# Computing a Q piece of a segment as one 16-head matmul group, so that only the last K is cut in two

## The chip, the cores and the metric

The kernel runs on one core of one Trainium2 chip. The metric is device time in microseconds (us). A "pair" below is one TensorE weight load with its matmul. Every single time here is of a run in the fast state (granted TensorE clock 0.989 to 0.999). Ratios are the mean time of a kernel's fast runs over that of the kernel before's fast runs on the same chip, so they are not quite the ratios of the medians that stand beside them. "The first chip" below is that of the first call, the one of before and after; its number is not on record, and three of before's four times and its trace existed before the changed kernel was shown, so that all of them ran on one chip is assumed. The kernel before itself took 922 to 925 us on the numbered chips and 933 us on the first; so kernels are compared through their ratio, and with kernels of the same call where possible.

## The reference, cut to what matters

An attention layer that runs over 64 segments one after the other, because the first 8 rows of a segment's input (the memory) are the output of the segment before; then a gated MLP over all rows, which the change does not touch.

```python
for s in range(n_seg):                               # 64 segments of 32 rows, D = 512
    h = jnp.concatenate([mem, xs], axis=1)           # 8 memory rows + 32 rows
    q = jnp.einsum('btd,dhe->bhte', h, Wq)           # 32 heads of 128
    k = jnp.einsum('btd,dhe->bhte', h, Wk)
    v = jnp.einsum('btd,dhe->bhte', h, Wv)
    scores = jnp.where(mask, jnp.einsum('bhqe,bhke->bhqk', q, k) * scale, -1e9)
    o = jnp.einsum('bhqk,bhke->bhqe', _softmax(scores), v)
    o = jnp.einsum('bhte,hed->btd', o, Wo)
    mem = o[:, :M, :].copy()                         # feeds the next segment
```

## The kernel before

A segment goes through these stages on TensorE: Q and K of all heads; scores of the heads 0 to 15 (half 0); V; scores of half 1; the sums of the softmax; PV of both halves; the output product; the memory rows, which are copied into the next segment's input `hT`. PV is the product of the softmax's weights with V. "Filler" below is Q, K and V work for rows of later segments that don't depend on the memory (lines 404 and 423); it is put where TensorE would otherwise wait. Q and K come in pieces. A piece is a run of matmuls into one PSUM bank (4 parts of the contraction times 4 column groups of the array), an eviction by ScalarE into `Tst`, and a transpose by VectorE into `QT` or `KT`:

```python
    QKP = ((0, 0, 8, (0, 1)), (1, 0, 4, (6, 7)), (1, 4, 4, (3, 2)))    # half, first pair of heads, pairs of heads, banks of Q and K

    def QK(s, piece, mi):                    # mi 0: Q, 1: K
        b, p0, np_, banks = piece
        ...
        h0, nh = 16 * b + 2 * p0, 2 * np_
        for dc in range(DC):                 # 4 parts of the contraction
            for c in range(4):               # 4 column groups of the array, side by side
                rhs = ws[:, dc, :].rearrange("p (h c i) -> p c h i", c=4, i=32)[:, c, h0:h0 + nh, :]
                pe(lambda e, ...: e.matmul(ps[32 * c:32 * c + 32, bank, 0:32 * nh], lhsT=hT[:, sl, dc, :], rhs=rhs,
                                           start=(dc == 0), stop=(dc == DC - 1), tile_position=(0, 32 * c)), ...)

    def QK_evac(piece, mi):
        ...
        act(lambda e: e.activation(out=st_..., in_=ps[:, bank, 0:64 * np_]..., func=ACT.Copy), ...)    # ScalarE: bank -> Tst
        ...
        dve(lambda e: e.transpose(out=dst, in_=src), ...)                                               # VectorE: Tst -> QT or KT

    for s in range(NSEG):
        ...
        for piece in QKP:
            for mi in range(2):
                QK(s, piece, mi)
                QK_evac(piece, mi)
        S_half(s, 0); sm_exp(0)
        V_half(s, 0, (0, 1, 2))
        S_half(s, 1)                         # needs the last K transpose
        sm_sums(0); sm_exp(1); sm_ln(0)
        V_half(s, 0, (3,)); V_evac(0, "dve")
        V_half(s, 1, gs=(0, 2)); V_evac(1, "dve", (0, 2))
        sm_sums(1); sm_rcp(0); sm_ln(1); sm_rcp(1)
        V_half(s, 1, gs=(2, 4)); V_evac(1, "act", (2, 4))
        sm_norm(0); sm_norm(1)
        ...                                  # PV, output product, memory rows (work of segment 0 alone is left out above)
```

A 16-head piece has 16 pairs of 512 columns; an 8-head piece 16 pairs of 256. The stage has 32 pairs of 512 and 64 of 256.

## Time and profile before

| | before |
|---|---|
| time, median (4 runs) | 933.11 us (930.78 to 934.89) |
| profiled execution | 925.72 us, core span 923.8 us |
| segment (first Q/K matmul to the next one's), median | 10.75 us |
| Q/K stage, first to last matmul start, median | 3.384 us |

Three places of the page: the busy time, the queue that brings the program, and the chain that ended last. In the queue's line stand the transfers, the MB and their share of 16 engines' span. "issue" in the chain is time in which the engine waited for nothing that the profile shows.

```profile
PE 875.5 (95%) x24038; PEld 572.1 (62%) x24045; DVE 458.0 (50%) x1098; ACT 461.4 (50%) x1281; POOL 155.3 (17%) x408
...
q8 instruction: 190, 3.11, 1.5%
...
PE 89%; DVE 3%; ACT 2%; DMA 2%; issue 2%; SPq 1%; POOL 0%; ACTq 0%
...
L477 PE MATMUL f_ps<-f_arena,f_hT 128*32 128x512 bf16 (+1 forms) x6144 | 233.9, 308 | 0.7 <-ACT f_hT L649 0.6
L489 ACT ACTIVATE f_Tst<-f_ps 128x256 bf16<-128x256 f32 (+1 forms) x384 | 155.7, 453 | 90.0 <-PE f_ps L477 70.9
```

TensorE bounds the kernel (busy for 95% of the span, 89% of the chain), and the Q/K matmuls (line 477) are its largest group (233.9 us).

### The profile page before, as it was taken

The page shows a single profiled execution, that of the slowest core. Times are in us where ns is not written, and L with a number is a line of the kernel's source. Part 1 is how long each engine was busy: PE and PEld are TensorE (multiplying, and loading weights), DVE is VectorE, ACT ScalarE, POOL GpSimd, SP SyncE. Part 2 cuts the span into 40 slices and gives each one's busy share as a digit, 9 for nine tenths or more (in the row PEclk, how much of TensorE's full clock was granted, in tenths as well). Part 3 has the DMA queues.
Part 4 walks back from the last instruction along what each step waited for, and adds up shares of the span by engine and source line. Part 5 has one row for each costly group of instructions (what it writes and reads, how often), then busy time and mean ns, then how long its engine had stood idle before and what let it go on. Part 6 is the DMA issues. An engine that isn't in the chain of part 4 may idle for free.

```text
span 923.8 us, 51830 instructions
## 1 busy us (share of the span) xinstructions
PE 875.5 (95%) x24038; PEld 572.1 (62%) x24045; DVE 458.0 (50%) x1098; ACT 461.4 (50%) x1281; POOL 155.3 (17%) x408
## 2 busy tenths in 40 slices
PE   6979999999999999999999999899989899999998
PEld 6756667776776777676676777566666544444443
DVE  3434555555554555455555555444445454453433
ACT  2436566666565665556565556555565655400000
POOL 1421111111111111111112111211111122200000
PEclk9999999999999999999999999999999999999999
DMA  9952322122303222222312020413132393021201
GB/s 321 376 154 59 66 52 62 42 50 64 73 19 75 44 56 44 50 61 38 50 44 68 26 78 22 118 27 84 39 55 51 68 269 120 1 98 49 84 12 36
DMA packets 103405, 71.69 MB, mean 78 GB/s; under 512 B 62120, under 2 KB 88688, under 8 KB 103184
## 3 DMA queue, kind: packets, MB, share of 16 engines
q1 hardware_dynamic: 102672, 68.06, 28.2%
q8 instruction: 190, 3.11, 1.5%
q14 instruction: 31, 0.25, 0.1%
q0 software_dynamic: 192, 0.20, 0.1%
q10 hardware_dynamic: 320, 0.07, 0.0%
HBM read 39.46 MB, written 18.61 MB: 63 GB/s over the span
## 4 chain that ended last, share of the span: by engine, by line
PE 89%; DVE 3%; ACT 2%; DMA 2%; issue 2%; SPq 1%; POOL 0%; ACTq 0%
PE f_ps L477 24%; PE f_ps L627 13%; PE f_ps L575 11%; PE f_ps L1025 10%; PE f_ps L404 6%; PE f_ps L594 3%; PE f_ps L671 3%; PE f_ps L423 3%; PE f_ps L987 3%; PE f_ps L1018 3%; PE f_ps L1095 2%; PE f_ps L646 2%; PE f_ps L520 2%; DVE f_V_sb L586 2%; PE f_ps L511 1%
## 5 line engine op out<-in xcount | busy, mean ns | idle before, releaser
L477 PE MATMUL f_ps<-f_arena,f_hT 128*32 128x512 bf16 (+1 forms) x6144 | 233.9, 308 | 0.7 <-ACT f_hT L649 0.6
L477 PEld LDWEIGHTS f_ps<-f_arena,f_hT 128*32 128x32 bf16 x6144 | 160.6, 97 | 77.1 <-ACT f_hT L649 16.6
L489 ACT ACTIVATE f_Tst<-f_ps 128x256 bf16<-128x256 f32 (+1 forms) x384 | 155.7, 453 | 90.0 <-PE f_ps L477 70.9
L575 PE MATMUL f_ps<-f_arena,f_hT 128*32 128x256 bf16 (+1 forms) x3072 | 142.2, 308 | 3.1 <-issue 3.0
L497 DVE STREAM_TRANSPOSE f_QT<-f_Tst 128x128 uint32<-128x128 uint32 (+1 forms) x192 | 65.8, 343 | 155.8 <-ACT f_Tst L489 155.8
L627 PE MATMUL f_ps<-f_arena,f_cT 128*32 128x384 bf16 (+1 forms) x4096 | 125.8, 274 | 9.3 <-ACT f_cT L613 8.7
L627 PEld LDWEIGHTS f_ps<-f_arena,f_cT 128*32 128x32 bf16 x4096 | 85.1, 97 | 52.0 <-ACT f_cT L613 20.9
L565 POOL TENSOR_TENSOR f_E_sb<-f_R_sb,f_E_sb 128x64 bf16<-128x64 f32 x128 | 43.8, 342 | 437.1 <-ACT f_R_sb L557 437.1
L1025 PE MATMUL f_ps<-f_arena 128*128 128x512 bf16 x448 | 101.3, 379 | 2.5 <-DVE f_arena L1031 1.6
L497 DVE STREAM_TRANSPOSE f_KT<-f_Tst 128x128 uint32<-128x128 uint32 (+1 forms) x192 | 68.4, 356 | 46.3 <-ACT f_Tst L489 46.3
L586 DVE TENSOR_SCALAR f_V_sb<-f_ps 128x512 bf16<-128x512 f32 (+1 forms) x128 | 65.9, 553 | 49.1 <-PE f_ps L575 49.0
L639 ACT ACTIVATE f_part<-f_ps 128x384 bf16<-128x384 f32 (+1 forms) x128 | 46.4, 384 | 83.9 <-PE f_ps L627 83.9
L575 PEld LDWEIGHTS f_ps<-f_arena,f_hT 128*32 128x32 bf16 x3072 | 68.7, 96 | 19.5 <-issue 5.1
L615 DVE TENSOR_SCALAR f_cT<-f_ps 128x320 bf16<-128x320 f32 x128 | 56.9, 486 | 47.1 <-PE f_ps L600 47.1
L1025 PEld LDWEIGHTS f_ps<-f_arena 128*128 128x128 bf16 x448 | 43.5, 98 | 56.0 <-DVE f_arena L1031 2.6
L404 PE MATMUL f_ps<-f_hTe,f_arena 128*128 128x128 bf16 x1024 | 72.6, 222 | 1.5 <-DMA f_arena<-in_A_Wk_dram 1.3
L613 ACT ACTIVATE f_cT<-f_ps 128x320 bf16<-128x320 f32 x128 | 49.0, 435 | 48.3 <-PE f_ps L600 48.3
L404 PEld LDWEIGHTS f_ps<-f_hTe,f_arena 128*128 128x128 bf16 x1024 | 58.5, 99 | 12.0 <-issue 10.1
L534 ACT ACTIVATE f_E_sb<-f_ps 128x224 bf16<-128x224 f32 x128 | 45.4, 355 | 35.8 <-PE f_ps L526 34.6
L594 PE MATMUL f_ps<-f_E_sb,f_V_sb 32*128 32x40 bf16 x2048 | 41.5, 178 | 8.9 <-DVE f_E_sb L561 5.7
L1031 DVE TENSOR_TENSOR f_arena<-f_ps,f_arena 128x512 f32<-128x512 f32 x28 | 19.3, 690 | 57.9 <-PE f_ps L1025 57.9
L557 ACT ACTIVATE f_R_sb<-f_R_sb 128x160 f32<-128x160 f32 x128 | 43.1, 337 | 4.4 <-ACT f_part L435 0.4
(103 smaller groups left out, 1052.6 us busy)
## 6 DMA issues: line engine op xcount, KB each, us to landing
wT_d<-f_wst SPq DMA_DIRECT2D x32, 256.0 KB, 3.4
f_arena<-wT_d SPq DMA_DIRECT2D x32, 256.0 KB, 4.6
f_arena<-in_A_Wq_dram SPq DMA_DIRECT2D x4, 1024.0 KB, 9.1
f_arena<-in_A_Wk_dram SPq DMA_DIRECT2D x4, 1024.0 KB, 14.3
f_arena<-in_A_Wv_dram SPq DMA_DIRECT2D x4, 1024.0 KB, 14.9
f_arena<-in_A_Wo_dram SPq DMA_DIRECT2D x4, 1024.0 KB, 13.7
f_Vx<-vext_d SPq DMA_DIRECT2D x62, 64.0 KB, 3.0
vext_d<-f_Vs SPq DMA_DIRECT2D x24, 128.0 KB, 2.2
```

What stands on the lines that cost most here:

```text
L404: pe(lambda e, h=h, dc=dc, hh=hh: e.matmul(ps[:, bank, hh * 128:(hh + 1) * 128], lhsT=ws[:, dc, h * DH:(h + 1) * DH], rhs=hTe[:, ck % 3, d ...
L477: pe(lambda e, dc=dc, c=c, rhs=rhs: e.matmul(ps[32 * c:32 * c + 32, bank, 0:32 * nh], lhsT=hT[:, sl, dc, :], rhs=rhs, start=(dc == 0), sto ...
L489: act(lambda e: e.activation(out=st_.rearrange("p (hp i r) -> p hp i r", i=32, r=2), in_=ps[:, bank, 0:64 * np_].rearrange("p (hp r i) -> ...
L497: dve(lambda e: e.transpose(out=dst, in_=src), reads=tok, writes=[(nm, b, k) for k in halves(b, p0, np_)])
L575: pe(lambda e, dc=dc, c=c, c0=c0: e.matmul(ps[32 * c:32 * c + 32, bank, 0:w], lhsT=hT[:, sl, dc, :], rhs=w_v[:, dc, c0:c0 + w], start=(dc ...
L586: dve(lambda e: e.tensor_scalar(out=dst, in0=src, scalar1=VSC, scalar2=None, op0=ALU.mult), reads=[PB(bank)], writes=tok)
L594: pe(lambda e, q=q, c=c, g=g, c0=c0: e.matmul(ps[:, PVB[c], c0:c0 + 40], lhsT=V_sb[q, b, g * 128:(g + 1) * 128], rhs=E_sb[q, b, g * 40:(g ...
L613: act(lambda e: e.activation(out=dst, in_=src, func=ACT.Copy, scale=UNSC), reads=[PB(PVB[c])], writes=[("cT", c)])
L615: dve(lambda e: e.tensor_scalar(out=dst, in0=src, scalar1=UNSC, scalar2=None, op0=ALU.mult), reads=[PB(PVB[c])], writes=[("cT", c)])
L627: pe(lambda e, h=h, g=g, i=i, b=b, c=c: e.matmul(ps[32 * g:32 * g + 32, bank, 0:d1 - d0], lhsT=cTh[:, i, 8:40], rhs=w_o[:, h, d0:d1], star ...
L639: act(lambda e: e.activation(out=part[:, s % 8, d0:d1], in_=ps[:, bank, 0:d1 - d0], func=ACT.Copy), reads=[PB(bank)], writes=[("part", s % ...
L1025: pe(lambda e: e.matmul(ps[:, bank, 0:TB], lhsT=z2[:, sc, fb * 128:(fb + 1) * 128], rhs=wTb[tb % 2][:, :, sc, :], start=(sc == 0), stop=(s ...
```

## The change

Its intent: the same columns in fewer instructions, none of the change in the stretch where the softmax's latency is exposed. The Q piece of half 1 becomes one 16-head piece; only the last K stays in two, so that the last eviction and transpose before the scores remain small (in before about 380 and 311 ns at 256 columns, 597 and 445 ns at 512). Per segment: 80 pairs in place of 96, 5 evictions and 5 transposes in place of 6, and no Q/K piece in bank 3.

```diff
-    QKP = ((0, 0, 8, (0, 1)), (1, 0, 4, (6, 7)), (1, 4, 4, (3, 2)))
+    QKP = ((0, 0, 8, 0, 0), (0, 0, 8, 1, 1), (1, 0, 8, 0, 6), (1, 0, 4, 1, 7), (1, 4, 4, 1, 2))
...
-    def QK(s, piece, mi):
-        b, p0, np_, banks = piece
+    def QK(s, piece):
+        b, p0, np_, mi, bank = piece
...
         for piece in QKP:
-            for mi in range(2):
-                QK(s, piece, mi)
-                lastop["qk"[mi]] = em.by_eng["pe"][-1]
-                QK_evac(piece, mi)
+            QK(s, piece)
+            lastop["qk"[piece[3]]] = em.by_eng["pe"][-1]
+            QK_evac(piece)
```

More of the change, by code (lines that the diff above doesn't have):

```diff
@@ L466, in fast_path @@
     VXB = 5
-    def QK(s, piece, mi):
-        b, p0, np_, banks = piece
+    def QK(s, piece):
+        b, p0, np_, mi, bank = piece
         ws = (w_q, w_k)[mi]
-        bank = banks[mi]
         sl = slot(s)
@@ L482, in halves, with QK_evac @@
         return range(p0 // 4, (p0 + np_) // 4)
-    def QK_evac(piece, mi):
-        b, p0, np_, banks = piece
-        bank = banks[mi]
+    def QK_evac(piece):
+        b, p0, np_, mi, bank = piece
         st_ = Tst[:, mi, 64 * p0:64 * (p0 + np_)]
```

## The prediction

> **What bounds the kernel.** The page's busy shares give PE 95% (875.5 of 923.8 us), ACT 50%, DVE 50%; the chain of waits that ended last is 89% PE. Most of the span is 64 serial segments (median 10.6 to 10.9 us from one segment's first Q/K matmul to the next one's). The granted clock is 0.998. PE's stream of columns, plus PE's waits inside a segment, set the time.
>
> **What the change does.** A segment's Q/K stage has 32 pairs of 512 columns and 64 of 256 before, 48 and 32 after. Columns are the same 32,768; 16 pairs go (1,024 of 24,038 matmuls), with one ScalarE eviction and one VectorE transpose a segment. The softmax, V, PV and output parts keep their order on every engine. The last piece (256-column K, eviction, transpose) keeps its size; only banks change, and those written next have been evicted long before.
>
> **Cost on PE, from the timeline's start times.** Four column groups run side by side: starts 3 to 4 ns apart inside a group of four, then one column sweep. A group of four takes about 217 ns at 512 columns and 109.2 ns at 256, so two 256 groups cost 218.4: the weight loads (about 97 ns each) are hidden. [...] Four 512 groups in place of eight 256 groups save 6 to 10 ns a segment. The "16 fewer pairs" are 17% of the stage's pairs but about 0.2% of its 3.38 us.
>
> **The eviction chain.** The second score half starts 55 ns after the last K transpose, about 40 ns after PE could have gone. In before, the last K eviction starts 51 ns after its last matmul ends: it waits only for PE, not for ScalarE's backlog. For after I estimate starts from the segment's first Q/K matmul with trace durations (eviction 512: 597 ns, 494 to the next; 256: about 380, 280 to the next; transpose 445 and 311[...]): Q eviction 2.83 us, first K half 3.32, last K 3.70 (before: 3.71); transposes 3.46, 3.83, 4.11 (before: last at 4.12). So the score half gains under 10 ns; the backlog that the change clears was hidden. ScalarE's and VectorE's saved work lies off the critical path. The later waits (PV on the normalised E, output product on the context eviction, memory rows on ScalarE) move along unchanged.
>
> **Sum.** 5 to 10 ns a segment x 64 = 0.3 to 0.6 us, below the 4 us spread of the three runs before.
>
> Predicted: 932.4 us, range 929.0 to 935.5. Faster by over 2%: 1%; within 2%: 98%; slower by over 2%: 1%.
>
> **What the profile would show.** Right: 23,014 matmuls; first to last Q/K matmul start falls by about 10 ns from 3.38 us; 320 Q/K evictions and transposes; ScalarE and VectorE each 4 to 10 us less busy with the span unchanged; last K eviction still about 50 ns after its matmuls; second score half at 4.48 us; median segment within 20 ns. Wrong: the Q/K stage shortens by over 50 ns (pairs had a price of their own), or the last transpose queues behind the larger Q transpose, which moves the second score half by up to 50 ns (+3 us, still within 2%).
>
> **What would make it wrong.** Instruction fetch on PE, if the scattered "issue" stalls (2% of the chain) scale with the number of instructions: about 1 us. The exposed transpose queue. [...]

The sum stands at 5 to 10 ns a segment, 0.3 to 0.6 us in all. Before's trace gives the steps from start to start: 216.7 ns for a group of four at 512 columns (mean; median 216), 109.2 ns at 256; for queued transposes 0.37 us after one of 128x256 uint32, 0.28 us after one of 128x128. The starts laid out above use only the first of these two.

## More of the kernel before

The experiments ran in calls of several kernels each, on different chips (named by number where known).

The program is fully unrolled: 24,038 matmuls stand one after the other in TensorE's instruction stream.

## The result, and the profile after

The changed kernel took 919.45 us (918.16 to 921.66, 4 runs) against 933.11 us: a ratio of 0.9858, 95% interval 0.9828 to 0.9887. That is within 2%, but 13 us below the predicted 932.4 and outside its range. The core spans of the profiled executions differ by less, 923.8 and 916.0 us.

The same lines of the page for the changed kernel:

```profile
PE 874.1 (95%) x23021; PEld 544.1 (59%) x23021; DVE 449.2 (49%) x1034; ACT 461.1 (50%) x1217; POOL 155.1 (17%) x408
...
q8 instruction: 182, 2.98, 1.4%
...
PE 92%; DVE 3%; ACT 2%; DMA 1%; issue 1%; SPq 0%; POOL 0%
...
L476 PE MATMUL f_ps<-f_arena,f_hT 128*32 128x512 bf16 (+1 forms) x5120 | 233.4, 337 | 0.7 <-ACT f_hT L647 0.7
L487 ACT ACTIVATE f_Tst<-f_ps 128x512 bf16<-128x512 f32 (+1 forms) x320 | 156.7, 510 | 88.5 <-PE f_ps L476 88.4
```

The Q/K matmuls take the same busy time (233.4 against 233.9 us), and so do the evictions. What has moved is "issue" in the chain, 2% to 1%, and the instruction transfers, 190 to 182: eight of 16,384 bytes less for the 1,024 pairs, 2,048 instructions, that were removed: 64 bytes an instruction.

I laid the two traces beside each other, with times from the first Q/K matmul of each segment (medians of the segments):

| | before | after | predicted for after |
|---|---|---|---|
| last Q/K matmul starts | 3.384 us | 3.374 us | about 10 ns earlier |
| eviction of the last K starts | 3.71 us | 3.70 us | 3.70 us |
| transpose of the last K starts | 4.12 us | 4.11 us | 4.11 us |
| second score half starts | 4.49 us | 4.48 us | 4.48 us |
| shortest segment | 10.556 us | 10.543 us | 5 to 10 ns less |
| median segment | 10.75 us | 10.58 us | within 20 ns |
| the 62 segments after the first, together | 671.5 us | 662.6 us | 0.3 to 0.6 us less |

Every step inside an undisturbed segment came out as laid out. But few segments of before were undisturbed. Sorted into kinds with the same side work, each segment's excess over the shortest of its kind adds up to 12.2 us before and 4.3 us after (other ways of sorting move this by some 0.3 us). So the gain is not in the segment's schedule; it lies in something that lengthens single segments at irregular places.

One such place in before, from the timeline. The columns are start, length, engine, line, operation, out and in with shapes, count, and in brackets how long the engine had been idle and what ended it:

```profile
369.62 0.11 PEld L575 LDWEIGHTS f_ps<-f_arena,f_hT 128*32 128x32 bf16 x4
...
369.65 0.28 PE L575 MATMUL f_ps<-f_arena,f_hT 128*32 128x256 bf16 x4
...
370.51 0.23 PEld L575 LDWEIGHTS f_ps<-f_arena,f_hT 128*32 128x32 bf16 x12 [0.79 <-issue]
370.51 0.51 PE L575 MATMUL f_ps<-f_arena,f_hT 128*32 128x256 bf16 x12 [0.58 <-issue]
```

This is a V quarter: 16 pairs of one kind, with no semaphore between them. Four go, then TensorE stands still for 0.8 us, then twelve go. No other engine holds it up.

Over the whole run such waits show in the list of waits of the weight loads. The columns are who waited, for what, us in total, times, and the longest. Before:

```profile
PEld f_ps L404 <- issue: 10.1, 41, 1.5
PEld f_ps L575 <- issue: 5.1, 8, 1.5
...
PEld f_ps L594 <- issue: 2.6, 6, 1.2
...
PEld f_ps L627 <- issue: 2.5, 10, 0.5
...
PEld f_ps L541 <- issue: 1.4, 3, 0.5
```

and after:

```profile
PEld f_ps L404 <- issue: 10.8, 43, 0.8
...
PEld f_ps L625 <- issue: 2.2, 10, 0.5
...
PEld f_ps L592 <- issue: 1.1, 2, 0.6
...
PEld f_ps L573 <- issue: 0.3, 1, 0.3
```

The first line of each (some 0.25 us a time, at filler matmuls that use the whole array after column tiles) is much the same in both, and so is that of line 627 (625 in the changed kernel); a wait that stays like this does not explain the gain. The other lines shown go from 9.1 to 1.4 us. All "issue" waits of the weight loads but the first line, those not shown included, go from 15.8 to 7.5 us.

I then numbered TensorE's trace records and looked where over 0.4 us pass from one record's start to the next one's, between 150 and 730 us, at an instruction that waits on no semaphore. These I call long stops; their lengths include the ordinary step from one record to the next. For before:

```
record number    16833 17345 19649 22465 22721 23489 25281 26049 26305 28353 36801 42177
modulo 256         193   193   193   193   193   193   193   193   193   193   193   193
```

All twelve stand a multiple of 256 instructions apart, and 256 instructions of 64 bytes are 16,384 bytes, the size of every one of the 190 transfers of the instruction queue (before has 48,223 TensorE records, 254 a transfer). The changed kernel has four such stops, all at 193 modulo 256 too. At the twelve stops of before, the block's transfer had landed 1.26 to 1.59 us before its first instruction ran, and 3.5 to 4.5 us (median 3.9) lay between the first instruction of the block before and that of the late one.

That gives theory A. TensorE's program is brought in blocks of 256 instructions, and where blocks are used up faster than the next ones come, TensorE stops. In the middle of the loop (with filler work) a segment of before has 722 TensorE records in about 10.7 us, so a block lasts 10.7 x 256/722 = 3.8 us on average: inside the range of 3.5 to 4.5 us that passed at the stops. After the change it is 690, 4.0 us a block. And some stretches are denser than the average. The range is not a limit for a single block: 36 of before's 149 blocks between 150 and 730 us took less than 3.5 us from start to start (the shortest 2.87), so blocks can also follow each other faster. What tells a late block is its landing. In the traces of before, the changed kernel, e1, e3 and e9 no block's first instruction started, in that stretch, less than 1.1 us after the last transfer had landed. All twelve stops of before stand at blocks whose transfer had landed less than 1.6 us before, and so do the long stops at block starts of all other traces but one (in e1, 2.1 us). Of all blocks, 64 of 149 had landed so late in before, and 24 of 144 in the changed kernel.

Most block starts made no long stop: 137 of the 149 between 150 and 730 us in before, and 140 of 144 in the changed kernel.

The rivals. Theory B: the sixth eviction and transpose cost the time. Theory C: the banks did, since a Q piece of before shared bank 3 with filler work. Theory D, which the prediction named: a pair has a price of its own on the array.

### The profile page after: what moved, and what is told of

Its sections match the earlier page's. It is cut to its first block, busy times and chain, and to the rows that moved or that the text cites. A ratio compares the mean times of both kernels' runs of the same rounds, so it can differ in the third digit from the quotient of the medians.

```text
span 916.0 us, 49661 instructions
## 1 busy us (share of the span) xinstructions
PE 874.1 (95%) x23021; PEld 544.1 (59%) x23021; DVE 449.2 (49%) x1034; ACT 461.1 (50%) x1217; POOL 155.1 (17%) x408
## 4 chain that ended last, share of the span: by engine, by line
PE 92%; DVE 3%; ACT 2%; DMA 1%; issue 1%; SPq 0%; POOL 0%
PE f_ps L476 24%; PE f_ps L625 13%; PE f_ps L573 11%; PE f_ps L1022 10%; PE f_ps L404 7%; PE f_ps L592 3%; PE f_ps L669 3%; PE f_ps L423 3%; PE f_ps L984 3%; PE f_ps L1015 3%; PE f_ps L1092 3%; PE f_ps L518 2%; DVE f_V_sb L584 2%; PE f_ps L644 2%; PE f_ps L509 1%; PE f_ps L598 1%
## 5 line engine op out<-in xcount | busy, mean ns | idle before, releaser
L476 PE MATMUL f_ps<-f_arena,f_hT 128*32 128x512 bf16 (+1 forms) x5120 | 233.4, 337 | 0.7 <-ACT f_hT L647 0.7
L487 ACT ACTIVATE f_Tst<-f_ps 128x512 bf16<-128x512 f32 (+1 forms) x320 | 156.7, 510 | 88.5 <-PE f_ps L476 88.4
L476 PEld LDWEIGHTS f_ps<-f_arena,f_hT 128*32 128x32 bf16 x5120 | 132.8, 97 | 104.1 <-ACT f_hT L647 16.2
L495 DVE STREAM_TRANSPOSE f_QT<-f_Tst 128x256 uint32<-128x256 uint32 x128 | 57.0, 445 | 181.7 <-ACT f_Tst L487 181.7
L573 PE MATMUL f_ps<-f_arena,f_hT 128*32 128x256 bf16 (+1 forms) x3072 | 140.1, 308 | 0.0
L495 DVE STREAM_TRANSPOSE f_KT<-f_Tst 128x128 uint32<-128x128 uint32 (+1 forms) x192 | 65.8, 343 | 27.7 <-ACT f_Tst L487 26.3
L573 PEld LDWEIGHTS f_ps<-f_arena,f_hT 128*32 128x32 bf16 x3072 | 67.2, 96 | 15.3 <-issue 0.3
L532 ACT ACTIVATE f_E_sb<-f_ps 128x224 bf16<-128x224 f32 x128 | 45.4, 355 | 35.8 <-PE f_ps L524 34.6
## 6 DMA issues: line engine op xcount, KB each, us to landing
f_arena<-in_A_Wo_dram SPq DMA_DIRECT2D x4, 1024.0 KB, 13.6
```

Of the source, the lines that this page charges most:

```text
L476: pe(lambda e, dc=dc, c=c, rhs=rhs: e.matmul(ps[32 * c:32 * c + 32, bank, 0:32 * nh], lhsT=hT[:, sl, dc, :], rhs=rhs, start=(dc == 0), sto ...
L487: act(lambda e: e.activation(out=st_.rearrange("p (hp i r) -> p hp i r", i=32, r=2), in_=ps[:, bank, 0:64 * np_].rearrange("p (hp r i) -> ...
L495: dve(lambda e: e.transpose(out=dst, in_=src), reads=tok, writes=[(nm, b, k) for k in halves(b, p0, np_)])
L573: pe(lambda e, dc=dc, c=c, c0=c0: e.matmul(ps[32 * c:32 * c + 32, bank, 0:w], lhsT=hT[:, sl, dc, :], rhs=w_v[:, dc, c0:c0 + w], start=(dc ...
```

## The experiments

Thirteen runs were made (e5 and e13 are the changed kernel itself). Stops are counted as above (over 0.4 us, no semaphore, 150 to 730 us, in the profiled execution). "wT" is the spatial weight of the MLP, which the kernel transposes by transfers in the background of the segment loop.

| run | chip | pairs in Q/K, evictions | instruction transfers | stops, us | us | ratio to before |
|---|---|---|---|---|---|---|
| before | | 96, 6 | 190 | 12, 7.5 | 933.11 | 1 |
| after | | 80, 5 | 182 | 4, 2.7 | 919.45 | 0.9858 |
| e1 pairs back | 12 | 96, 5 | 190 | 8, 5.1 | 924.39 | 1.0019 |
| e2 six evictions | 12 | 80, 6 | 182 | 3, 2.3 | 916.64 | 0.9944 |
| e3 128 pairs | 12 | 128, 5 | 206 | 45, 35.8 | 966.49 | 1.0494 |
| e4 before, no wT | 12 | 96, 6 | 190 | 0 | 919.32 | 0.9966 |
| e5 after again | 7 | 80, 5 | 182 | 4, 2.9 | 917.16 | 0.9917 |
| e6 no-operations | 7 | 80, 5 | 182 | 5, 3.1 | 918.73 | 0.9933 |
| e7 V whole | 7 | 80, 5 | 174 | 1, 1.0 | 918.70 | 0.9942 |
| e8 K whole | 7 | 64, 4 | 174 | 2, 1.1 | 936.01 | 1.0128 |
| e9 96 more loads | 12 | 80, 5 | 206 | 45, 37.3 | 967.76 | 1.0483 |
| e10 after, no wT | 12 | 80, 5 | 182 | 0 | 916.07 | 0.9937 |
| e11 memory rows in 4 | 12 | 80, 5 | 176 | 5, 3.9 | 924.59 | 1.0029 |
| e12 V split one to three | 11 | 80, 5 | 174 | 2, 1.5 | 920.69 | 0.9968 |
| e13 after again | 11 | 80, 5 | 182 | 5, 3.0 | 917.96 | 0.9933 |

Before took 922.2 to 922.4 us on chip 12, 924.6 on chip 7 and 922.7 on chip 11. Every stop in the table but one of e11's five stands at the first instruction of a block of 256.

### e1: the pairs back, everything else of the change kept

```diff
-        for dc in range(DC):
-            for c in range(4):
+        cuts = ((0, 8), (8, 16)) if (b, mi) == (1, 0) else ((0, nh),)
+        for u0, u1 in cuts:                  # two column halves of the same bank
+            for dc in range(DC):
+                for c in range(4):
```

> The changed kernel, but its second Q piece is computed as two 256-column halves into its one bank: 96 pairs a segment as before, with the 5 evictions, 5 transposes and the banks of the changed kernel. Theory A (TensorE is short of instructions: its program is brought in 16 KB blocks of 256 instructions, and a block that is used up faster than the next one arrives stops it): back to the time of before, 928 to 935 us. Theory B (fewer evictions and transposes gave the time): stays at 918 to 921. Theory C (the banks gave it, as no Q piece shares bank 3 with the filler any more): stays at 918 to 921.

Measured: 924.39 us against 922.22 us for before on this chip, ratio 1.0019 (0.9992 to 1.0046). The absolute numbers were expected for a chip on which before takes 933; in the ratio, with the 16 pairs back, the whole gain is gone, although evictions, transposes and banks are those of the changed kernel. Theories B and C each expected the gain to stay.

### e2: six evictions and transposes, 80 pairs

```diff
+        if (b, mi) == (1, 0):                # the Q piece of half 1: evict and transpose 256 columns at a time
+            for k in range(2):
+                QK_evac1((b, 4 * k, 4, mi, bank), 256 * k)
+        else:
+            QK_evac1(piece, 0)
```

> The changed kernel with its 80 pairs and banks, but the second Q piece is evicted and transposed in two halves, so 6 evictions and 6 transposes a segment as before. Theory A: stays at 918 to 922 us. Theory B: back to 930 to 935. Theory C: stays at 918 to 922.

Measured: 916.64 us, ratio 0.9944 (0.9924 to 0.9963). The gain stays with the old number of evictions. e1 and e2 ran side by side: 16 pairs make 7.8 us, the eviction nothing that shows. Theory B falls.

### e3: 128 pairs

```diff
+        cuts = ((0, 8), (8, 16)) if nh == 16 else ((0, nh),)    # every 16-head piece in two column halves
```

> The changed kernel with every Q and K piece computed in 256-column halves: 128 pairs a segment, 32 more than before, evictions, transposes and banks as in the changed kernel. Array time alone, at 1 to 2.5 ns for each extra group of four, would add 12 groups x 2 ns x 64 = 1.5 us: 920 to 922 (theories B and C). Theory A: well above before, 940 to 970 us, with more stops of TensorE that have no semaphore behind them, each at the first instruction of a block of 256.

Measured: 966.49 us, ratio 1.0494 (1.0450 to 1.0537). The page and the waits of TensorE:

```profile
q8 instruction: 206, 3.38, 1.5%
...
PE 89%; issue 4%; DVE 2%; ACT 2%; DMA 1%; SPq 0%; POOL 0%
```

```profile
PE f_ps L576 <- issue: 7.3, 15, 1.0
...
PE f_ps L404 <- issue: 4.0, 5, 1.3
PE f_ps L521 <- issue: 3.0, 6, 0.7
PE f_ps L595 <- issue: 3.0, 7, 0.9
```

The stops fall on V (line 576), filler (404), scores (521) and PV (595), that is, on whatever stands 256 instructions further on; only 5 of the 45 long stops are on the Q/K line where the pairs were added. All 45 long stops stand at 193 modulo 256. The shortest Q/K stage of the run is 3.391 us against 3.362: the array price of 48 more pairs is 29 ns a segment, 2 us in all. The dose is steep: 16 more pairs than the changed kernel cost about 0.8%, 48 more cost 5.5%. In the middle of the loop a segment now has 786 records, which without stops would be 3.5 us a block (an estimate: 256/786 of the 10.7 us above); the trace has 3.77 us on average. Of the 154 blocks between 150 and 730 us, 110 had landed less than 1.6 us before their first instruction, and 45 stopped TensorE for over 0.4 us.

### e4: before, without the background transfers of the spatial weight

```diff
-        if s % 2 == 1 and s // 2 < NWT:
-            wT_piece(s // 2)
+        if s == 1:
+            wT_piece(0)
...
-        sp(lambda e, t=t: e.dma_start(wTb[tb % 2][:, t, :, :], wT_d[8 * tb + t]), reads=[("wTd", 8 * tb + t)],
+        sp(lambda e, t=t: e.dma_start(wTb[tb % 2][:, t, :, :], wT_d[0]), reads=[("wTd", 0)],
```

> The kernel before, with 31 of the 32 transposing loads and stores of the spatial weight taken out of the segment loop (its later loads read the first piece; the result is wrong on purpose). Is the block of instructions late because other transfers hold its queue up? If so, the 16 KB transfers (0.88 to 1.83 us in the trace) get shorter and the time falls to 915 to 925. If the round trip is a fixed latency, the time stays at 929 to 935 and the transfers of instructions keep their spread.

Measured: 919.32 us against 922.22, ratio 0.9966 (0.9944 to 0.9988), and no long stop at all. The result is wrong on purpose. The time fell inside the first band, but that band had been set for a chip where before takes 933, and the instruction transfers grew only a little shorter (median 1.04 us, against 1.10 in e1, the run with 190 transfers on the same chip). So other transfers make some blocks late (8 long stops in e1, none here); the transfer itself, at about 1 us, is the smaller part of the 3.5 to 4.5 us between blocks at a stop.

### e6 and e9: instructions that compute nothing

e6 put 96 no-operations a segment on TensorE's queue:

```diff
+            if piece[:4] == (1, 0, 4, 1):
+                for _ in range(96):
+                    pe(lambda e: e.nop(nofuse=True))
             QK(s, piece)
```

> The changed kernel with 96 no-operation instructions a segment on TensorE's queue, just before the first half of the last K: no weight is loaded and no column computed by them. A segment then has as many instructions as the run with 128 pairs had. Theory A: near that run's ratio to before (1.049), 945 to 975 us, with stops at every 256th instruction. If pairs cost array time of their own, no-operations cost nothing: as the changed kernel, 916 to 922.

Measured: 918.73 us, ratio 0.9933 (0.9914 to 0.9951). This looks like a blow to theory A, but the experiment failed. Its trace has 49,661 instructions and 182 instruction transfers, exactly those of the changed kernel: the no-operations were not in the program that ran. The run says only how well the changed kernel repeats (0.9917 for the changed kernel itself). The lesson is to check in the trace that an edit arrived.

e9 took weight loads instead, which do arrive:

```diff
             for c in range(4):
                 ...
+                for _ in range(2 if nh == 16 else 0):
+                    pe(lambda e, dc=dc, c=c: e.ldweights(hT[:, sl, dc, :], tile_position=(0, 32 * c)), ...)
                 pe(lambda e, ...: e.matmul(...))
```

> The run with no-operations said nothing: its trace has the changed kernel's 49,661 instructions and 182 instruction transfers, so they never reached the chip. In their place: the changed kernel with two more weight loads before each of the 48 matmuls of 512 columns in the Q/K stage, 96 a segment, of weights that nothing is computed with; no matmul, column, eviction or transpose is added. Instructions a segment as in the run with 128 pairs. Theory A: 206 instruction transfers, stops at every 256th instruction, a ratio to before of 1.03 to 1.06 if the loads themselves are hidden under the columns. If only matmuls and their columns cost: 0.99 to 0.995. If the loads are not hidden, the first-to-last start of the Q/K stage (3.37 us) grows and tells it.

Measured: 967.76 us, ratio 1.0483 (1.0453 to 1.0512), as e3's 1.0494. From its page:

```profile
PE 892.1 (92%) x23014; PEld 595.2 (62%) x29165; DVE 450.1 (47%) x1034; ACT 463.5 (48%) x1217; POOL 155.4 (16%) x408
...
q8 instruction: 206, 3.38, 1.5%
...
PE 89%; issue 4%; DVE 3%; ACT 2%; DMA 1%; POOL 0%; SPq 0%
```

Matmuls, columns and evictions are those of the changed kernel; the stream is 6,144 instructions longer, as e3's is. The shortest Q/K stage is 3.361 us against 3.362 in the changed kernel, so the loads are hidden under the columns where they stand. And yet the kernel is some 5% slower, with 45 long stops, all at the first instruction of a block, most of them elsewhere. This is the run that separates the number of instructions from the work in them: theory D falls, theory A holds.

How much of the time do the block starts explain? For this check I took every block start between 60 and 740 us that waits on no semaphore, and the time from the record before it, less the usual time between the same two instructions elsewhere. The sums are 13.6 us in before and 5.6 after, 11.1 in e1, 4.8 in e2, 47.7 in e3 and 53.6 in e9. So the block starts alone hold the 7.8 us between the spans of before and after, 6.3 of the 8.1 us between e1 and e2, 42.9 of the 47.3 us between e3 and e2, and 48.8 of the 53.1 us between e9 and e2.

### e10: the changed kernel without the background transfers

The edit is e4's, on the changed kernel.

> The changed kernel without 31 of the 32 transposing loads and stores of the spatial weight in its segment loop (wrong on purpose). In the kernel before, this took the stops over 0.4 us away. Theory A with other transfers as the reason for a late block: the changed kernel's last stops go too, 2 to 4 us under the changed kernel; ratio to before 0.986 to 0.99. If the stops left are not made by these transfers: as the changed kernel, 0.991.

Measured: 916.07 us, ratio 0.9937 (0.9917 to 0.9957); no long stop is left. The ratio is that of the changed kernel on other chips (0.9917, 0.9933) and of e2 on this one (0.9944): the stops went, as expected, but the 2 to 4 us did not show clearly. The 62 segments after the first took 659.7 us (663.1 and 663.4 in e5 and e13), which would be the expected 3 us, on other chips; against e2 on this chip (661.6 us) it is 2 us. Without the background transfers the 16 pairs still cost something: e4 took 3 us more than e10 (919.32 against 916.07, on this chip), and its block starts hold 2.1 us more (4.7 against 2.6, counted as above). They were run at other times.

### e5 and e13: the changed kernel on other chips

> The changed kernel itself, beside before on one chip: on the chip of the first four runs before took 922 us, not 933, so the size of the gain may belong to the chip. If the gain is the stops of TensorE at the ends of instruction blocks, it should follow the stops: on a chip where before takes 922 us, 916 to 918 (a ratio of about 0.994, as the run with six evictions had); where before takes 933, 919 to 921.

> The changed kernel on the chip of the run beside it, for comparison on the same chip. If the gain follows the stops of before, its ratio to before goes with before's time: about 0.994 where before takes 922 us, 0.986 where it takes 933.

Measured: on chip 7, 917.16 us against 924.57, ratio 0.9917 (0.9903 to 0.9932); on chip 11, 917.96 us against 922.67, ratio 0.9933 (0.9898 to 0.9967). The time of the changed kernel hardly depends on the chip (917 to 919 us); that of before does (922 to 933). So the gain is 14 us on the first chip and 5 to 7 us on the others. On the first chip the instruction transfers were longer (median 1.14 us before, 1.12 after; 1.00 to 1.10 in all later runs). That fits theory A, but I could not choose chips, and the link between the two is argued, not shown.

### e8: fewer instructions, but in the wrong place

```diff
-    ... (1, 0, 4, 1, 7), (1, 4, 4, 1, 2))
+    ... (1, 0, 8, 1, 7))                     # the last K in one piece too
```

> The changed kernel with the last K in one 16-head piece too: 64 pairs a segment, 5 to 4 evictions. Theory A alone says faster still (2 to 4 us). But the last eviction (597 ns in place of 380) and transpose (445 in place of 311) then stand between the last Q/K matmul and the second score half, which waits for nothing else: estimated 0.35 us a segment, 20 us in all. Net 932 to 940 us if before takes 922.

Measured: 936.01 us, ratio 1.0128 (1.0109 to 1.0147), with the stops nearly gone (2). The wait of the second score half for the last K transpose, first in the changed kernel's trace, then in e8's:

```profile
PEld f_ps L518 <- DVE f_KT L495: 15.1, 63, 0.2
```

```profile
PEld f_ps L518 <- DVE f_KT L495: 36.7, 63, 0.6
```

It grew by 21.6 us (20 had been estimated from the eviction's and transpose's durations). That is why the change leaves the last K in two pieces: the chain from the last matmul to the scores is exposed, and the instructions saved are worth less.

### e7, e12 and e11: trying to beat both kernels

e7 takes 16 pairs out of the V stage, e12 is a second try at it.

```diff
...                                          # V_evac: both parts of half 1 from one bank
-        V_half(s, 1, gs=(0, 2)); V_evac(1, "dve", (0, 2))
+        V_half(s, 1, (0, 1))                 # all 512 columns, first half of the contraction
         sm_sums(1); sm_rcp(0); sm_ln(1); sm_rcp(1)
-        V_half(s, 1, gs=(2, 4)); V_evac(1, "act", (2, 4))
-        sm_norm(0); sm_norm(1)
+        V_half(s, 1, (2, 3))
+        sm_norm(0)
+        V_evac(1, "dve", (0, 2)); V_evac(1, "act", (2, 4))    # e12: (0, 1) and (1, 4)
+        sm_norm(1)
```

> The changed kernel with the second V half in one bank: two column quarters of 256 become one of 512, so 16 more pairs go, now from the softmax stretch; the second sums stand between its two halves of the contraction, where they stood before; one half of the bank is evicted by VectorE after the first normalisation, the other by ScalarE behind it. Theory A: the remaining stops shrink, 2 to 6 us under the changed kernel (ratio 0.993 to 0.998 of it), if the later evictions do not delay the second PV half; if they do, up to 8 us over it.

> The run with the second V half in one bank lost its stops but gained 55 ns a segment: the second PV half waited for the second eviction from that bank, which may not start before the first has read it. Now VectorE takes one head group in four first (128 columns) and ScalarE the other three, so ScalarE starts about 0.15 us earlier and the second normalisation too. Estimate: PV ends 50 ns earlier than in that run, segments as short as the changed kernel's 10.56 us and no stops: 3 to 5 us under the changed kernel in the same rounds (ratio to before 0.986 to 0.990). If the ScalarE eviction of 384 columns ends later than the two of 256 did, no better than the changed kernel.

Measured: e7 918.70 us, ratio 0.9942 (0.9925 to 0.9958), beside 0.9917 for the changed kernel; e12 920.69 us, ratio 0.9968 (0.9939 to 0.9997), beside 0.9933. The stops went (1 and 2 left), but the shortest segment grew from 10.54 to 10.60 us in both, 60 ns x 64 = 4 us, about what the stops had cost. In both, the two evictions of V from one bank follow each other (the kernel lets no two engines read a bank at once); e12's other split did not shorten the segment. e12's six runs lie within 1.6 us of one another, and those of before beside them within 10.5 us; but e7's lie no closer (3.5 us) than the changed kernel's beside it (3.5) and before's (3.9), so that fewer stops make a kernel repeat better is not shown.

e11 takes 12 pairs out of the memory rows by using the whole array:

```diff
-        for dc in range(DC):
-            for c in range(4):               # 32 columns of weights each, one column group of the array
-                pe(... matmul(ps[32 * c:32 * c + 32, GB, ...], lhsT=part[:, s % 8, c0:c0 + 32], rhs=G_sb[:, :], ..., tile_position=(0, 32 * c)))
+        for dc in range(DC):                 # 128 columns of weights
+            pe(... matmul(ps[:, GB, ...], lhsT=part[:, s % 8, dc * 128:dc * 128 + 128], rhs=G_sb[:, :], ...))
```

> The changed kernel with the memory rows taken by 4 matmuls with 128-column weights in place of 16 with 32-column weights: 12 more pairs go, at a place where TensorE waits for an eviction anyway. Theory A: fewer blocks, fewer stops, 1 to 3 us under the changed kernel (ratio to before 0.988 to 0.991). If changing from column tiles to the whole array costs time here, slower than the changed kernel by up to 0.1 us a segment (6 us).

Measured: 924.59 us, ratio 1.0029 (1.0010 to 1.0048), slower than the changed kernel's 0.9917 and 0.9933 on other chips. The single run of before in this call took 926.05 us, so that e11 is also slower than before is not shown. The loads of this stage (first the changed kernel, then e11):

```profile
PEld f_ps L644 <- ACT f_part L637: 11.7, 47, 0.3
```

```profile
PEld f_ps L642 <- ACT f_part L637: 19.2, 49, 0.7
```

The idle time ahead of these loads grew by 7.5 us, 0.12 us a segment, as the second branch of the expectation had it. The list puts it down to the eviction, whose work did not change. In the changed kernel, where the whole-array loads of the filler (line 404) follow column tiles, the weight loads sat idle for 211 ns before them (median of 39), between two column tiles for 0 (median); that the change from column tiles to the whole array makes the 7.5 us is an estimate from this, not shown separately. Nor did its stops fall as theory A expected: 5 (3.9 us) with 176 instruction transfers, against 3 (2.3 us) with 182 in e2 on this chip. So fewer instructions in all do not always mean fewer stops; why not here stays open.

No version beat the changed kernel.

## Why the prediction was wrong

**What was right.** TensorE bounds the kernel; Q/K columns cost the same; the stage shortens by 10 ns (3.384 to 3.374 us), and two groups of four at 256 columns cost within 2 ns of what one at 512 does (2 x 109.2 = 218.4 ns against means of 216.7 in before and 216.4 in the changed kernel). The eviction chain was laid out to within 10 ns, the instruction counts were right (23,014 matmuls and a few), and so was "ScalarE's and VectorE's saved work lies off the critical path" (e2: ratio 0.9944 with the sixth eviction and transpose). VectorE's busy time fell as predicted (458.0 to 449.2 us). ScalarE's, predicted to fall by 4 to 10 us, did not (461.4 and 461.1): one 512-column eviction kept it busy as long as two of 256 that overlap (all Q/K evictions 155.7 us before, 156.7 after).

**The step that failed** is the sum: "5 to 10 ns a segment x 64 = 0.3 to 0.6 us". It holds for an undisturbed segment, which is 10 ns shorter, and takes every segment for an undisturbed one. The term for the others stood under what would make it wrong: "Instruction fetch on PE, if the scattered 'issue' stalls (2% of the chain) scale with the number of instructions: about 1 us." The mechanism was named and mis-sized. It measured 7.9 us in the pair of traces (segment excess 12.2 to 4.3 us; the long stops alone 7.5 to 2.7 us) and, through e1 against e2, 7.8 us for the 16 pairs (of which 6.3 us stand at block starts in the traces). The size was wrong because the stalls were scaled in proportion to the instructions. They are not in proportion: 4% fewer instructions took the excess at block starts from 13.6 to 5.6 us, and 9% more than before (e3) took it to 47.7 us. A block that comes in time costs next to nothing (in before, 94 of the 162 block starts summed above had a transfer that landed 1.6 us or more ahead: median excess 0, 1.1 of the 13.6 us; the other 68 hold 12.5 us), and many of before's came barely in time: 64 of the 149 between 150 and 730 us landed less than 1.6 us before their first instruction. The trace of before had what was needed: 190 transfers of 16 KB about 3.9 us apart, stops only at the starts of blocks of 256 instructions, and 722 instructions in a segment of 10.7 us. That the time still fell within 2%, as it gave at 98%, is no credit to its sum: the measured 13.7 us are over twenty times that.

**The tests that were named.** "Wrong: the Q/K stage shortens by over 50 ns (pairs had a price of their own)" did not happen: the price of the pairs is paid wherever a late block begins (in e3, 40 of the 45 long stops stand on other lines), so the stage where they were removed could not show it. The queue of transposes played no part (the last starts at 4.11 us, as laid out), nor did the banks (e1 has those of the changed kernel and a ratio of 1.0019).

**What stays open.** On the first chip the four timed runs of before took 931 to 935 us and its profiled execution 925.7; the traces show 7.8 us of the 13.7 us difference of the medians, and the other 6 us stand in executions without a trace. More stops of the same kind would explain them; no run shows it. Also open is what starts a block's transfer, what part of the 3.5 to 4.5 us between blocks at a stop is other transfers (e4 and e10 show that they contribute), and what part is fixed.

## What to carry to other kernels

In a long unrolled program, count TensorE's instructions per microsecond as well as its columns. If a run of identical instructions stands still with "issue" as the only reason, number the records: stops at a fixed place modulo 256 meant here that the program itself came too late, and then merging small matmuls gained more than their array time, even where the removed ones were well hidden (7.8 us between e1 and e2, against 10 ns a segment or 0.6 us of array time). Cut instructions where no latency is exposed: the last piece before a dependent stage should stay small (e8: 21.6 us more of waiting), and a saved pair was no gain where the merged result was evicted later (e7, e12: shortest segment 60 ns longer).
